# Partials of two weight groups in the attention's PSUM banks, and two half-chunks of attention moved to later units

## The chip, the cores and the metric

One Trainium2 chip, one core of it. The metric is device time in microseconds (us): the median of the runs, of which three are shown for the kernel before. The profile is of one further execution.

## What is computed

The reference, cut to what matters here:

```python
state = alpha[:, :, t, :, None] * state + einsum('bhd,bhe->bhde', k[:, :, t], v[:, :, t])
y[:, :, t] = einsum('bhd,bhde->bhe', q[:, :, t], state)      # 4 x 8 heads, 768 steps, 48 x 48
h = x @ w_in                                                   # 3072 tokens, 384 -> 2048
g = (a0 + a1*h + a2*h2 + a3*h3) / (1 + |b0|*|h| + |b1|*h2 + 1e-6)
x = g @ w_out                                                  # 2048 -> 384
```

After that comes a second network (384 -> 1024 -> 384) with a softmax and a normalisation between its two products. Everything is fp32; each fp32 factor is split into a high and a low part (hi, lo), and a product is three matmuls: hi by hi, hi by lo, lo by hi.

## The kernel before

**Units.** The 768 steps are cut into 6 chunks of 128 steps (512 tokens). The first network runs 16 units per chunk, one for each 128 of the 2048 hidden columns, 96 in all: unit u has chunk c = u // 16 and place f = u % 16. `m_up(u)` (L583) does 9 matmuls (L590) into one of three PSUM banks `hp` and computes the rational function on ScalarE (ACT), VectorE (DVE) and GpSimd (POOL); the last DVE instruction that reads the bank is `fin[u]` (L614 in even units below 24, L621 in the others), and the bank is free for `m_up(u + 3)` after it. `m_down(u - 4)` (L627) does 9 matmuls (L636) into the three `x2p` banks.

**Halves.** Attention is done in 12 halves; half i serves chunk i // 2, columns 256 * (i % 2) of its input `xt`. Halves 0 and 1 are done ahead of unit 0. For a later half, `a_dve(i)` (L300) prepares q and k in six steps on DVE (transposes, two scans, two products) and writes them to DRAM (`qk_d`, `kb_d`); `a_move_qk(i)` (L273) reads them back into `qks`, `a_move(i)` (L279) into `kns`, with v into `vns`. All three of these buffers are single. `a_pe(i)` (L411) then has five steps: scores of the first and of the second pair (L420, a copy on ACT, a triangular mask on POOL L428), y (L444, copied on ACT to the high part and subtracted on DVE to the low part of `xt`, L471), an empty step, and u (L483, with the state's update on DVE L493 and L494). Its scores, y and u come out of the pool `ps_a`, whose tag "at" has two banks. m_up(16), the first unit of chunk 1, needs y of halves 2 and 3.

`half_steps(i)` (L850) takes one step of a_pe(i) and two of a_dve(i + 1), then a_move_qk(i + 1) and the loads of half i + 2, per unit, and ends with a_enter(i + 1). It begins at f = 2 and at f = 10 of every chunk: half 2 at unit 2, half 3 at unit 10, half 4 at unit 18.

**Weights of the first network.** They come in 4 groups (`w1_group`, L550) of 7 pieces: three of `moe_w_in` (128x512 values) and four of `moe_w_out` (128x384). They arrive as 64-bit floats, and `split_w` (L507) turns each piece into fp32 by three integer instructions on DVE: L535 (shift and mask of the high word into the partial `gi`), L538 (sign bit into `gi`), L539 (low word and `gi` into `fi`). ACT then makes the high part (L545) and POOL the low part (L546). Where the partial `gi` lives is `stage["bank"]`:

```python
if stage["bank"] == "x2":
    fp = ps_x2p.tile([128, NTOK], F32, name="fp", tag=f"x2p{x % KT}")
elif stage["bank"] == "at":
    fp = ps_ap.tile([128, NTOK], F32, name="fp", tag="at")
else:
    fp = ft
```

Groups 0 and 1 are done ahead of unit 0 with "x2" (PSUM). Groups 2 and 3 are done beside units 0 to 3 and 4 to 7, two pieces a unit, with the partial in SBUF (`fp = ft`). Their raw words land in two buffers `st`. Group n is first used by m_up(4n). The second network's weights (`w2_split`, 14 pieces, "at") are split one at a time from unit 15 on, at f % 8 of 0 and 7.

**Order.** A planner orders the instructions of each engine when the program is built, and the engines then run them in that order. `issue_after` keeps an instruction behind another one of its engine: `pin(n)` (L842) holds a half's step at unit u behind m_up(u)'s last matmul on TensorE (PE), and behind fin[u - n] on DVE, n = 2. Transfers go through SyncE's queue (SP), in order, and are not pinned.

Of the kernel before, what the change touches and what calls it, by code (L numbers as in the profile page):

```python
# [10 lines left out]
I64 = mybir.dt.int64  # L11
# [12 lines left out]
def _run(*gens):  # L24
    for g in gens:
        for _ in g:
            pass
# [3 lines left out]
def kernel(  # L31
# [23 lines left out]
    NTOK = B * CH  # L55
# [19 lines left out]
    GP = 2  # L75
# [5 lines left out]
    SKIP = (5, 7, 11)  # L81
    AHEAD = 3
    LATE = 2
    U2, IDLE = NF1 - 1, (0, NF1 // 2 - 1)
    assert (B, H, D, CH) == (4, 8, 48, 128)

    const = ctx.enter_context(tc.tile_pool(name="const", bufs=1, side="left"))
# [65 lines left out]
    def network(fast):  # L153
# [38 lines left out]
        def borrow(n, o, dims):  # L192
            if n not in lent:
                lent[n] = moe_pool.tile([128, GW], F32, name=f"lent{n}", tag=f"g{n}")
            size = 1
            for d in dims:
                size *= d
            t = lent[n][:, o:o + size]
            if len(dims) == 1:
                return t  # L200
            nm = "abcd"[:len(dims)]
            return t.rearrange(f"p ({' '.join(nm)}) -> p {' '.join(nm)}", **dict(zip(nm, dims)))
# [197 lines left out]
        def a_prep(i):  # L400
            if i >= NPE:
                yield from a_dve(i)

        def a_enter(i):
            if i < NPE:
                v_load(i)
                yield from a_turn(i)
            else:
                yield from a_move(i)
# [92 lines left out]
        wi = {}  # L502
        wo = {}

        stage = {"n": 0, "wide": False, "bank": None}

        def split_w(src, hi, lo, scale=None):  # L507
            keep = None
            if hi is None:
                keep, raw = lo, moe_pool.tile([128, NTOK], I64, name="st", tag="st", bufs=2)  # L510
                n = src.shape[1]
                both = raw[:].bitcast(F32R)
                hi, lo = both[:, :n], both[:, n:2 * n]
            n = src.shape[1]
            x = stage["n"]
            stage["n"] += 1
            ft = moe_pool.tile([128, NTOK], F32, name="ft", tag="ft", bufs=2)
# [6 lines that stand above are left out]
            if src.dtype == I64:  # L524
                if keep is not None:
                    st = raw
                elif stage["wide"] and x % 6 not in (0, 2):
                    st = borrow(2, 2048 + 1024 * (0, 0, 0, 1, 2, 3)[x % 6], [2 * NTOK]).bitcast(I64)
                else:
                    st = moe_pool.tile([128, NTOK], I64, name="st", tag="st", bufs=2)  # L530
                nc.sync.dma_start(out=st[:, :n], in_=src)
                w32 = st[:, :n].bitcast(I32).rearrange("p (n t) -> p n t", t=2)
                fi = ft[:, :n].bitcast(I32)
                gi = fp[:, :n].bitcast(I32)
                nc.vector.tensor_scalar(  # L535
                    gi, w32[:, :, 1], 3, 0x3FFFFFF8, ALU.logical_shift_left, ALU.bitwise_and
                )
                nc.vector.scalar_tensor_tensor(gi, w32[:, :, 1], -0x40000000, gi, ALU.bitwise_and, ALU.bitwise_or)  # L538
                nc.vector.scalar_tensor_tensor(fi, w32[:, :, 0], 29, gi, ALU.logical_shift_right, ALU.bitwise_or)  # L539
            else:  # L540
                nc.sync.dma_start(out=ft[:, :n], in_=src)
            f = ft[:, :n]
            if scale is not None:
                nc.scalar.activation(f, f, AF.Copy, scale=scale)
            nc.scalar.activation(hi, f, AF.Copy)  # L545
            nc.gpsimd.tensor_tensor(lo, f, hi.bitcast(F32), ALU.subtract)  # L546
            if keep is not None:
                nc.sync.dma_start(out=keep, in_=both[:, :2 * n].bitcast(F32).rearrange("p (x n) -> p x n", x=2))
# [102 lines left out]
        def w2_split():  # L651
            nc.sync.dma_start(out=gln, in_=moe2_g_ln.rearrange("(f p) -> p f", p=128))
            for o in range(0, DF2, 512):
                for kt in range(KT):
                    split_w(moe2_w_in[128 * kt:128 * kt + 128, o:o + 512], None, w2i_d[:, :, kt, o:o + 512])
                    yield
            for f in range(NF2):
                split_w(moe2_w_out[128 * f:128 * f + 128, :], None, w2o_d[:, :, f, :], scale=gln[:, f:f + 1])
                yield
# [144 lines left out]
        if fast:  # L804
            stage["wide"] = True
            stage["bank"] = "x2"
            pre = w1_group(0)
            _run(a_load(0))
            take(pre, PRE[0])
            v_load(0)  # L810
            consts()
            take(pre, PRE[1])
            _run(a_load(1))
            take(pre, PRE[2])
            v_load(1)
            take(pre, PRE[3])
            nc.gpsimd.memset(Sbd, 0.0)
            _run(a_turn(0), a_pe(0), a_turn(1), a_pe(1), pre)
            clear()
            pre = w1_group(1)  # L820
            take(pre, NA)
            _run(a_load(2, ("ra", "rk")))
            with tc.issue_after(marks[0, 1].ins):
                _run(a_prep(2))
            _run(a_move_qk(2))
            _run(a_enter(2), pre)
            _run(a_load(3, ("ra", "rk")))
            stage["wide"] = False
            stage["bank"] = ""
        else:  # L830
            for n in range(NG):
                _run(w1_group(n))
            x_load(0)
# [16 lines left out]
        def half_steps(i):  # L850
            gp = a_pe(i)
            gd = chain(a_prep(i + 1), a_move_qk(i + 1) if i + 1 >= NPE else iter(()), a_load(i + 2, ("ra", "rk")) if i + 2 < NH and i + 1 >= NPE else iter(())) if i + 1 < NH else iter(())
            while True:
                with pin(GP):
                    a = next(gp, "end")
                with pin(GS):
                    b = next(gd, "end")
                    if b != "end":
                        b = next(gd, "end")
                if a == "end" and b == "end":  # L860
                    if i + 1 < NH:
                        _run(a_enter(i + 1))
                        if i + 2 < NH and i + 1 < NPE:
                            _run(a_load(i + 2))
                    return
                yield

        split2 = w2_split() if fast else iter(())
        side = iter(())
        tail = None  # L870
        prep = iter(())
        for u in range(NU + LAG):
            c, f = divmod(u, NF1)
            now[0] = u
            if f % (NF1 // 2) == LATE and u < NU:
                _run(side)
                i = 2 * c + 2 + f // (NF1 // 2)
                side = half_steps(i) if fast and i < NH else iter(())
            if u < NU:
                if f == 0 and c == NCH - 1:  # L880
                    if fast:
                        judge(moe_pool)
                    open2()
                    tail = chain(w2_load("i"), n_load(0), w2_load("o"))
                if f == 0 and c and not fast:
                    x_load(c)
                if fast and u < NF1:
                    if f % 4 == 0:
                        _run(prep)
                        prep = w1_group(f // 4 + 2) if f < 8 else iter(())  # L890
                    with later(G1):
                        take(prep, 1)
                m_up(u)
                if fast and u < NF1:
                    with later(G1):
                        take(prep, 1)
            if u == NU:
                _run(n_load(1))
            take(side, 1)
            if u >= U2 and f % (NF1 // 2) in IDLE:  # L900
                stage["bank"] = "at"
                with later(G2):
                    take(split2, 1)
            if tail is not None:
                _run(split2)
                take(tail, 2)
            if u >= LAG:
                m_down(u - LAG)
            if u - NU + NF1 in EARLY:
                n_tile(EARLY.index(u - NU + NF1))  # L910
                if len(EARLY) == B and u - NU + NF1 == EARLY[-1]:
                    n_turn(0)
# [141 lines left out]
```

## Time and profile before

| | |
|---|---|
| median of 3 runs | 786.02 us (785.37 to 788.82) |
| the profiled execution | 786.76 us, its span 784.9 us |
| PE matmuls busy | 730.2 us, 93% |
| DVE busy | 639.8 us, 82% |
| ACT busy | 534.5 us, 68% |
| POOL busy | 359.9 us, 46% |
| DMA | 101.74 MB, mean 130 GB/s |

Times in the rows are from the start of the span. Unit 0 begins at 56.8 us (its m_up), unit 16 at 169.3. Two instructions of one engine may overlap by some 0.1 us, so that a sum of single durations is a little longer than the busy time.

### The profile page before, as it was taken

How to read it: one execution, taken by the hardware profiler on the slowest of the kernel's cores; microseconds unless marked ns; L12 is line 12 of the kernel's file. 1: busy time of each engine (PE TensorE's matmuls, PEld its weight loads, DVE VectorE, ACT ScalarE, POOL GpSimd, SP SyncE). 2: the span in 40 equal slices, each digit the busy share in tenths (PEclk: the TensorE clock that was granted, in tenths of full speed). 3: DMA queues.
4: the chain of work that ended last, by engine and by line, in shares of the span. 5: the costliest groups of instructions: out<-in, count | busy, mean ns of one | idle time of the engine just before them, and what ended most of it. 6: DMA issues, size and time to landing. Idle time of an engine off the chain costs nothing.

```text
span 784.9 us, 13904 instructions
## 1 busy us (share of the span) xinstructions
PE 730.2 (93%) x4976; PEld 605.3 (77%) x4976; DVE 639.8 (82%) x1110; ACT 534.5 (68%) x983; POOL 359.9 (46%) x306
## 2 busy tenths in 40 slices
PE   4775896999999999999999999999999999999996
PEld 3654674778887788777878788888888989988996
DVE  5999999989899998989898966567887688777640
ACT  2245656779886888788978888788865555555541
POOL 3256677766755344444554433243233433352322
PEclk9767699899999999999999999999999999999998
DMA  7865547373858175536736250640024353542552
GB/s 172 239 201 174 142 154 158 114 182 115 189 167 208 57 196 134 146 83 208 157 121 122 82 121 2 228 175 0 1 82 101 115 120 90 140 102 57 139 121 72
DMA packets 87278, 101.74 MB, mean 130 GB/s; under 512 B 34464, under 2 KB 63136, under 8 KB 87200
## 3 DMA queue, kind: packets, MB, share of 16 engines
q1 hardware_dynamic: 87104, 100.67, 48.5%
q8 instruction: 41, 0.67, 0.4%
q14 instruction: 37, 0.30, 0.1%
q10 hardware_dynamic: 96, 0.10, 0.0%
HBM read 60.59 MB, written 27.56 MB: 112 GB/s over the span
## 4 chain that ended last, share of the span: by engine, by line
DVE 28%; PE 17%; ACT 13%; issue 5%; SPq 4%; DMA 4%; POOL 1%; ACTq 0%; DVEq 0%; POOLq 0%
PE x2p L636 6%; PE hp L590 6%; DVE room L750 3%; SPq L760 3%; DVE room L733 2%; PE op L774 2%; ACT jk L735 2%; DVE p L616 2%; DVE hp L620 2%; DVE w L619 2%; DVE sm L729 2%; DMA room<-room 2%; DMA rq<-in_q_dram 2%; DVE room L748 2%; PE h L710 2%
## 5 line engine op out<-in xcount | busy, mean ns | idle before, releaser
L590 PE MATMUL hp<-xt,g 128*128 128x512 f32 x864 | 225.0, 402 | 9.5 <-DVE alT L302 4.0
L624 POOL TENSOR_TENSOR gl<-p,gh 128x512 fp32r<-128x512 f32 x96 | 127.9, 1332 | 190.2 <-ACT gh L623 104.1
L590 PEld LDWEIGHTS hp<-xt,g 128*128 128x128 f32 x864 | 163.2, 192 | 50.0 <-DVE p L621 5.0
L636 PE MATMUL x2p<-gh,g 128*128 128x512 f32 x576 | 197.5, 397 | 2.8 <-ACT x2e L644 2.1
L636 PEld LDWEIGHTS x2p<-gh,g 128*128 128x128 f32 x576 | 108.6, 189 | 30.5 <-ACT x2e L644 4.7
L636 PE MATMUL x2p<-gl,g 128*128 128x512 f32 x288 | 113.6, 394 | 1.8 <-POOL gl L624 1.8
L774 PE MATMUL op<-w2oh,room 128*128 128x384 f32 x384 | 101.8, 339 | 1.2 <-DVE room L766 0.6
L766 POOL TENSOR_TENSOR room<-room,room 128x1024 fp32r<-128x1024 f32 x22 | 54.6, 2484 | 101.1 <-ACT room L765 79.7
L619 DVE SCALAR_TENSOR_TENSOR w<-w,co,hp 128x512 f32<-128x512 f32 x84 | 62.0, 738 | 44.2 <-ACT hp L618 43.3
L710 PE MATMUL h<-w2ih,x 128*128 128x512 f32 x288 | 90.7, 394 | 0.0
L597 ACT ACTIVATE p<-hp,co 128x512 f32<-128x512 f32 x96 | 65.9, 687 | 13.0 <-POOL gl L624 12.8
L618 ACT ACTIVATE hp<-ah 128x512 f32<-128x512 f32 x84 | 50.1, 596 | 32.8 <-DVE p L616 31.6
L774 PEld LDWEIGHTS op<-w2oh,room 128*128 128x128 f32 x384 | 70.1, 188 | 2.8 <-DVE room L766 1.0
L616 DVE SCALAR_TENSOR_TENSOR p<-p,co,hp 128x512 f32<-128x512 f32 x84 | 61.8, 736 | 10.2 <-ACT p L597 9.9
L598 ACT ACTIVATE w<-ah,co 128x512 f32<-128x512 f32 x96 | 69.4, 724 | 0.7 <-DVE hp L620 0.3
L595 ACT ACTIVATE ah<-hp 128x512 f32<-128x512 f32 x96 | 56.5, 589 | 13.7 <-PE hp L590 13.6
L636 PEld LDWEIGHTS x2p<-gl,g 128*128 128x128 f32 x288 | 54.2, 188 | 15.0 <-POOL gl L624 3.1
L623 ACT ACTIVATE gh<-p 128x512 fp32r<-128x512 f32 x96 | 59.9, 624 | 7.8 <-PE x2p L636 2.7
L774 PE MATMUL op<-w2ol,room 128*128 128x384 f32 x192 | 65.0, 339 | 0.0
L710 PEld LDWEIGHTS h<-w2ih,x 128*128 128x128 f32 x288 | 53.9, 188 | 11.7
L621 DVE SCALAR_TENSOR_TENSOR p<-p,co,hp 128x512 f32<-128x512 f32 x84 | 61.9, 737 | 1.1
L617 ACT ACTIVATE ah<-w,co 128x512 f32<-128x512 f32 x84 | 60.5, 721 | 1.2
(168 smaller groups left out, 1274.8 us busy)
## 6 DMA issues: line engine op xcount, KB each, us to landing
room<-room SPq DMA_DIRECT2D x96, 128.0 KB, 2.4
qk_d<-qk SPq DMA_DIRECT2D x10, 771.0 KB, 4.4
st<-in_moe_w_in_dram SPq DMA_DIRECT2D x15, 512.0 KB, 4.6
st<-in_moe_w_out_dram SPq DMA_DIRECT2D x18, 384.0 KB, 3.5
qks<-qk_d SPq DMA_DIRECT2D x20, 257.0 KB, 5.2
x<-x_d SPq DMA_DIRECT2D x18, 256.0 KB, 3.4
out_dram<-o SPq DMA_DIRECT2D x94, 48.0 KB, 1.6
ra<-in_alpha_dram SPq DMA_DIRECT2D x44, 96.0 KB, 2.3
```

The costliest lines, as they stand in the source:

```text
L590: last["PE", u] = nc.tensor.matmul(hp, lhsT=w[:, kt, 128 * o:128 * o + 128], rhs=xts[c][:, kt, xx, :], start=(kt == 0 and w is hi and xx = ...
L597: nc.scalar.activation(p, hp, AF.Square, bias=co[:, 7:8])
L598: nc.scalar.activation(w, ah, AF.Square, bias=co[:, 6:7])
L616: nc.vector.scalar_tensor_tensor(p, p, a1, hp, ALU.add, ALU.mult)
L617: nc.scalar.activation(ah, w, AF.Ln, bias=rest)
L619: nc.vector.scalar_tensor_tensor(w, w, rest, hp, ALU.add, ALU.mult)
L621: fin[u] = nc.vector.scalar_tensor_tensor(p, p, a0, hp, ALU.add, ALU.mult)
L623: last["ACT", u] = nc.scalar.activation(gh, p, AF.Copy)
L624: last["POOL", u] = nc.gpsimd.tensor_tensor(gl, p, gh[:].bitcast(F32), ALU.subtract)
L636: nc.tensor.matmul(x2ps[c][d], lhsT=w[:, o, 128 * d:128 * d + 128], rhs=gg, start=(f == 0 and w is hi and gg is gh), stop=(f == NF1 - 1 an ...
L710: nc.tensor.matmul(hp[:, 512 * n:512 * n + 512], lhsT=x2s[c][:, kt, x, CH * b:CH * b + CH], rhs=w2[w][:, kt, 512 * n:512 * n + 512], start ...
L774: nc.tensor.matmul(op, lhsT=x[:, 128 * f:128 * f + 128], rhs=w2[w][:, f, :], start=(f == 0 and x is hi and w == "oh"), stop=(f == NF2 - 1 ...
```

## The change

The partials of groups 2 and 3 go to the two "at" banks; group 2's raw words also land in four places of the buffer that group 3 takes later (`borrow(3, ...)`). The steps at units 2 to 11 are written anew (`first_steps`): a_dve(3) goes on one step a unit from unit 2, the scores of half 2 come at units 7 and 8, its y at 9 and its u at 11. Half 3 begins at unit 12 in place of 10, so that its y is at unit 14, its u at 16, and a_dve(4) at units 12 to 14. The second network's splits begin at unit 23 in place of 15.

```diff
-    U2, IDLE = NF1 - 1, (0, NF1 // 2 - 1)
+    FIRST = 10
+    U2, IDLE = NF1 + NF1 // 2 - 1, (0, NF1 // 2 - 1)
...
+                elif stage["near"] and x % 6 not in (0, 2):
+                    st = borrow(3, 2048 + 1024 * (0, 0, 0, 1, 2, 3)[x % 6], [2 * NTOK]).bitcast(I64)
...
-            stage["bank"] = ""
+            stage["near"] = True
+            stage["bank"] = "at"
...
+        def first_steps():
+            gd, gp = a_prep(3), a_pe(2)
+            for n in range(FIRST):
+                if n >= 5:
+                    with pin(GP):
+                        next(gp, "end")
+                with pin(GS):
+                    next(gd, "end")
+                    if n == FIRST - 2:
+                        _run(a_move_qk(3))
+                if n == FIRST - 1:
+                    _run(gp, a_enter(3), a_load(4, ("ra", "rk")))
+                yield
...
-            if f % (NF1 // 2) == LATE and u < NU:
+            if f in ((LATE, LATE + FIRST) if c == 0 else (LATE, LATE + NF1 // 2)) and u < NU:
                 _run(side)
                 i = 2 * c + 2 + f // (NF1 // 2)
-                side = half_steps(i) if fast and i < NH else iter(())
+                side = iter(()) if not fast or i >= NH else first_steps() if i == 2 else half_steps(i)
...
                     if f % 4 == 0:
                         _run(prep)
+                        if f:
+                            stage["near"] = False
                         prep = w1_group(f // 4 + 2) if f < 8 else iter(())
...
             if u >= U2 and f % (NF1 // 2) in IDLE:
-                stage["bank"] = "at"
                 with later(G2):
                     take(split2, 1)
```

## Rows read from the trace of the kernel before

**Rows 1.** The page's 40 slices: PE and DVE busy tenths, granted clock.

```profile
PE   4775896999999999999999999999999999999996
DVE  5999999989899998989898966567887688777640
PEclk9767699899999999999999999999999999999998
```

**Rows 2.** Windows, all engines: us, busy of PE, PEld, DVE, ACT, POOL, PEclk, DMA, GB/s.

```profile
56.80:169.30 112.50, 91.86 (x655) 70.69 (x656) 108.99 (x167) 71.59 (x133) 77.28 (x63) 0.86 0.57 153
169.30:600.00 430.70, 424.36 (x2995) 342.12 (x2994) 363.67 (x586) 353.47 (x638) 196.08 (x176) 1.00 0.45 122
```

**Rows 3.** Timeline of PE: start us, us, what, idle before and its releaser.

```profile
80.88 2.04 PE L420 MATMUL sc<-qks 48*128 48x128 f32 x8 [10.74 <-DMA qks<-qk_d]
...
109.21 1.14 PE L483 MATMUL u<-vns,kns 128*64 128x48 f32 x32
...
136.75 4.21 PE L590 MATMUL hp<-xt,g 128*128 128x512 f32 x9 [4.02 <-DVE alT L302]
...
153.85 1.13 PE L444 MATMUL y<-A,vns 128*32 128x128 f32 x31
...
169.34 2.22 PE L590 MATMUL hp<-xt,g 128*128 128x512 f32 x9
```

**Rows 4.** Timeline of DVE, the same columns.

```profile
67.38 0.40 DVE L535 TENSOR_SCALAR ft<-st 128x512 int32<-128x512 int32 x1
...
74.61 1.11 DVE L496 TENSOR_TENSOR Sbd<-u,end 48x384 f32<-48x384 f32 x2
...
79.91 0.68 DVE L614 SCALAR_TENSOR_TENSOR p<-w,hp 128x512 f32<-128x512 f32 x1
...
84.15 0.34 DVE L535 TENSOR_SCALAR ft<-st 128x384 int32<-128x384 int32 x1
...
136.02 0.67 DVE L614 SCALAR_TENSOR_TENSOR p<-w,hp 128x512 f32<-128x512 f32 x1
...
157.39 0.66 DVE L290 STREAM_TRANSPOSE qk<-rq 128x256 f32<-128x256 f32 x1
...
159.97 1.01 DVE L471 TENSOR_TENSOR xt<-y,xt 128x512 fp32r<-128x512 f32 x2
```

**Rows 5.** Windows of lines 535, 538, 539 in turn: us, DVE busy, PEclk, DMA, GB/s.

```profile
67.38:136.69 69.31, 9.17 (x12) 0.87 0.63 166
...
67.38:136.69 69.31, 12.92 (x12) 0.87 0.63 166
...
67.38:136.69 69.31, 11.83 (x12) 0.87 0.63 166
```

**Rows 6.** Groups by form, DVE, 160 to 460 us: busy us, mean ns, idle before.

```profile
L538 DVE SCALAR_TENSOR_TENSOR fp<-st,fp 128x384 int32<-128x384 int32 x8 | 4.5, 559 | 0.2
L535 DVE TENSOR_SCALAR fp<-st 128x384 int32<-128x384 int32 x8 | 4.5, 558 | 0.2
L539 DVE SCALAR_TENSOR_TENSOR ft<-st,fp 128x384 int32<-128x384 int32 x8 | 4.4, 552 | 0.2
L535 DVE TENSOR_SCALAR fp<-st 128x512 int32<-128x512 int32 x6 | 4.1, 691 | 0.5 <-DMA st<-in_moe_w_in_dram 0.4
L538 DVE SCALAR_TENSOR_TENSOR fp<-st,fp 128x512 int32<-128x512 int32 x6 | 4.1, 690 | 0.1
L539 DVE SCALAR_TENSOR_TENSOR ft<-st,fp 128x512 int32<-128x512 int32 x6 | 4.1, 682 | 0.1
```

**Rows 7.** Timeline of SP's queue: start us, us, issue.

```profile
118.66 0.43 SPq L348 DMA_DIRECT2D vns<-in_v_dram  x1
...
163.80 1.72 SPq L276 DMA_DIRECT2D qks<-qk_d  x4
```

**Rows 8.** DMA issues: queue, KB each, median us from issue to landing.

```profile
qks<-qk_d SPq DMA_DIRECT2D x20, 257.0 KB, 5.2
...
vns<-in_v_dram SPq DMA_DIRECT2D x22, 192.0 KB, 6.2
```

More of the change, by code (lines that the diff above doesn't have):

```diff
@@ L503, in network @@
         wo = {}
-        stage = {"n": 0, "wide": False, "bank": None}
+        stage = {"n": 0, "wide": False, "near": False, "bank": None}
         def split_w(src, hi, lo, scale=None):
```

## The prediction

> **What bounds the kernel now.** I begin with the slices. From the second on PE is below 9 tenths until about the eighth, while DVE stands at 8 or 9 all along; behind that PE is at 9 until the end [rows 1]. The windows make this sharper. From m_up(0) to m_up(16) PE is busy for 91.9 of 112.5 us at a mean granted clock of 0.86 (a mix of 1.2 and 2.4 GHz), DVE for 109.0. From there to 600 us PE is busy for 424.4 of 430.7 us at full clock [rows 2]. So the ramp in front of unit 16 is DVE's, and what follows is PE's. A microsecond taken out of the ramp moves everything behind it; one taken off DVE later moves next to nothing, and I cost it at nothing.
>
> Where does DVE hold PE up? The timeline of PE has two long gaps. The first, 10.74 us before 80.88, is put down to the transfer that brings half 2's q and k [rows 3]. It looks like the stall that this change removes, but it is worth little: the next unit in the queue, m_up(3), needs the bank of unit 0, whose fin[0] (L614) runs from 79.91 to 80.6 [rows 4]. Without the transfer PE would stand until 80.6 all the same. The second gap, 4.02 us, ends at 136.75 with m_up(11) [rows 3]. It needs the bank of unit 8, and fin[8] ends at 136.7 [rows 4]: DVE again. From there on PE is almost gapless, since m_up(11) to m_up(16) take 32.6 us. So the ramp has two parts: up to fin[8] DVE's queue sets the time, after it PE's work does.
>
> **The change part by part.** *The partials.* Between 67.38 us and fin[8], 12 of the 14 pieces of groups 2 and 3 are split: six of 512 values, six of 384. The three lines take 9.17 + 12.92 + 11.83 = 33.9 us there [rows 5]. With the partial in PSUM the later w2 pieces, of the same shapes and types, take 0.691 + 0.690 + 0.682 = 2.06 us at 512 and 0.558 + 0.559 + 0.552 = 1.67 at 384 [rows 6]. Six of each: 12.4 + 10.0 = 22.4 us. That is **11.5 us less** on the engine that sets this part, and I take all of it, because DVE is busy for 97% of the ramp [rows 2]. The bounds: 0, if DVE merely idles where it was busy; and 11.5 and the 4.0 us gap and the 3 to 4 us that PE runs at half clock behind it (m_up(11) takes 4.21 us, m_up(16) 2.22 [rows 3]), together some 19. The two pieces after fin[8] lie beside PE's own work: nothing.
>
> Here a rule speaks against the change. The row first: an SBUF L535 that meets no delay takes 0.40 us at 512 and 0.34 at 384 [rows 4], less than the 0.691 and 0.558 in PSUM [rows 6]; but the twelve of the ramp took 9.17 us, 0.76 each [rows 5], so most were held up. By the fast rows alone L535 would have been 6 x 0.40 + 6 x 0.34 = 4.4 us and becomes 7.5, 3.1 longer in place of 1.7 shorter, and the sum would be 11.5 - 4.8 = 6.7. That is a rival below. The Trainium skill, "VectorE: DVE Perf Modes", section "Why PSUM operands drop a tier", states that a PSUM operand keeps a one-input instruction out of the mode that uses both SBUF read ports. These rows agree, but they also show that here the mode was mostly not had.
>
> *Scores, y and u of half 2 to units 7 to 11.* PE's work is the same. PE alone would not be the bound: from 70.1 us to m_up(11) it has 8 up and 7 down units of 2.2 us [rows 3], 33 us, and half 2's small matmuls. These are at most 8 us of scores (32 at the half-clock rate of 8 in 2.04), 4 of y (112 at 31 in 1.13) and 1 of u. So 46 us at the most, up to 116, before 136.7 - 11.5 = 125.2. Half 2's y and state update on DVE (L471, 1.01 us [rows 4], and L493) come about at fin[8] in place of before it: 0 to 2 us of gain, counted as 0. a_dve(3), one step a unit, still ends at unit 7, before fin[8]: nothing. Its qk transfer has until unit 12: nothing.
>
> *The "at" banks.* Two banks now serve the splits beside half 1's last tiles, which are let go by L496 at 74.61 to 75.7 [rows 4]; the first split of group 2 was at 67.38. If it had to wait for L496, DVE would lose up to 7 us, filled in part by units 0 and 1. Usually one of the two banks is free: I take 0, bound 7.
>
> *Raw words in four more places.* Group 2's loads go out earlier. DVE had no lack of work: 0.
>
> *Half 3 two units later.* Three transfers get closer to their readers, and PE's queue is in order, so a wait there holds all the matmuls behind it. A unit of PE is 4.4 us (two nines at 2.2).
> - xt for m_up(16): before, y ended at 155.0 [rows 3] and the low part on DVE at 161.0 [rows 4], 6.0 us later. Now m_down(10), m_up(15) and m_down(11) lie between, 6.6 us: 0, bound 4 if DVE is late.
> - v for y(3): u(2) ended at 110.35 [rows 3], the second vns transfer was issued at 118.66 [rows 7] and takes 6.2 [rows 8], so 125.3, 15 us later. Now three units and the scores lie between, 13.2 + 2.3 = 15.5 us: 0, bound 5.
> - q and k for half 4's scores, at unit 18 as before while a_dve(4) has moved by two units: its last transposes ended at 158.0 [rows 4], the qks issues at 165.5 [rows 7], and landing takes 5.2 [rows 8]: 170.7, 12.7 us. DVE ended a_dve(4) two units behind its place in the code; two units behind unit 14 is m_up(16), and up to the scores PE has two units, u(3) and m_up(18): 8.8 + 1.1 + 2.2 = 12.1 us. **A wait of about 1 us**, bounds 0 and 10.7, what the half-2 scores waited [rows 3].
>
> *w2 splits from unit 23.* They leave units 15 and 16 and end at unit 72, before their readers at unit 80: work moved under PE's, 0.
>
> **Sum.** -11.5 + 1 = -10.5 us. The profiled execution took 786.76 us, 0.74 above the median of the three runs, so 776.3 of its kind, 775.5 against the median.
>
> **The rivals.**
> 1. *More comes back.* The gap at m_up(11) and the half clock behind it shrink as well, and half 2's y and u leave the part before fin[8]: -19 us, 767. For: PE's bound is 9 us below DVE's. Against: DVE has 97% of the ramp, and a shorter queue on it idles more.
> 2. *The tier.* L535's delay is only handed on to the next instruction with two SBUF operands (the scans, L320), so 6.7 us come off, less the 1: 780. For: the fast L535 rows. Against: the w2 pieces run beside POOL work too. The rule is the one of the Trainium skill, "VectorE: DVE Perf Modes", section "Why PSUM operands drop a tier".
> 3. *Given back, or not done.* Banks not free (7), or the two waits at y(3) and unit 16 (5 and 4): 11.5 is met by 7 to 11.5 and the time is 783 to 786. For: lead times of 15 us against 15.5. Against: no unit after 16 shows such waits with the usual distances.
> 4. *Slower: scores wait for their transfer, twice.* The scores of half 3 at unit 12 and of half 4 at unit 18 each stand as long as half 2's did, 10.74 us, with all later units behind them in PE's queue: 21.5 - 11.5 = +10, 796. It decides from where both waits exceed 11.5 us together. For: that wait did happen at the one place where the transfer had no lead, and half 4 loses two units of lead. Against: half 3 has five units between a_dve(3) and its scores.
>
> **How the numbers follow.** Chances: the forecast 0.50, rival 1 0.15, rival 2 0.10, rival 3 0.14, rival 4 0.11. The range from 764 to 784 holds the forecast's own 771 to 780, rivals 1 and 2 and the lower part of 3; the rest and rival 4 are left out. A measurement of this kernel can tell a change of about 0.5%, 3.9 us: faster is below 782.1. Forecast, rivals 1 and 2 and a little of 3 are faster, 0.78; most of 3 is the same, 0.12; 4 is slower, 0.10, but for its mildest part.
>
> **What would show it.** Right: lines 535, 538 and 539 of all 28 pieces at 1.7 and 2.1 us a piece; DVE's busy time in the ramp about 12 us shorter; fin[8] at about 125 and m_up(16) near 159 us; from there to the end the same length as before. Scores of half 4 with a wait of a microsecond or so. Wrong: L538 and L539 at 0.7 us but DVE idle before them; waits on qks, vns or xt of more than 3 us at units 12 to 18; m_up(16) earlier and the stretch behind it longer.

## The result: 0.8% slower, and the profile after

Over ten runs each the median is 792.88 us after the change and 786.2 before; the ratio is **1.0082, with a 95% interval of 1.006 to 1.0104**. The forecast was 775.5 us. The profiled execution took 793.11 us, its span 791.3. In the changed file lines are one to three higher: L538, L541 and L542 are the split's three instructions, L421 the scores, L445 y, L471 and L472 the high and low part of xt, L593 m_up, L639 m_down, L598 ACT's first instruction of a unit.

The page of the changed kernel, its span and slices, against [rows 1]:

```profile
span 791.3 us, 13930 instructions
...
PE   4776879998999999999999989999999999999996
...
DVE  5999999808889999889898966566887698777630
```

PE's seventh slice went from 6 to 9 and its sixth from 9 to 7. DVE's ninth slice, from 158 to 178 us, went from 8 to 0: DVE stands nearly still on both sides of m_up(16). The windows of the changed kernel (us; busy of PE, PEld, DVE, ACT, POOL; PEclk, DMA, GB/s) have PE a little busier and DVE less busy in the first 169.3 us [rows 2]. I cut the ramp at m_up(11) and m_up(16):

```profile
56.80:169.30 112.50, 95.11 (x580) 75.60 (x583) 96.96 (x163) 76.35 (x138) 72.43 (x66) 0.89 0.44 121
...
56.80:124.09 67.29, 51.23 (x213) 40.84 (x214) 65.54 (x113) 45.67 (x82) 44.93 (x38) 0.82 0.47 134
124.09:172.80 48.71, 46.69 (x444) 37.07 (x442) 31.44 (x52) 31.33 (x59) 27.87 (x29) 1.00 0.41 114
```

DVE's busy time in the old ramp's window went from 109.0 to 97.0 us, in part because it stands idle at the end of that window. But from m_up(11) to m_up(16) it now takes 48.7 us in place of 32.6, and DVE is busy for 31.4 of them. It was busy for nearly all of it before:

```profile
136.75:169.34 32.59, 31.02 (x254) 23.95 (x255) 31.12 (x51) 24.41 (x46) 22.13 (x20) 0.92 0.52 142
```

The table gives the start of ACT's first instruction of a unit (us; in brackets the difference from the kernel before), read off each trace; the last three columns are experiments that come below.

```
unit   before   after            e1               e6               e10
  4     96.0     86.9 ( -9.1)     86.6 ( -9.4)     86.0 (-10.0)     86.9 ( -9.1)
  8    126.0    114.6 (-11.5)    115.3 (-10.8)    110.7 (-15.3)    114.5 (-11.5)
 12    152.7    133.1 (-19.6)    140.2 (-12.5)    141.3 (-11.4)    135.7 (-17.1)
 14    164.8    144.7 (-20.1)    153.0 (-11.8)    151.0 (-13.7)    147.3 (-17.5)
 16    173.6    178.4 ( +4.8)    167.7 ( -5.9)    160.4 (-13.1)    176.2 ( +2.6)
 32    254.8    259.8 ( +5.0)    249.9 ( -4.9)    243.4 (-11.4)    257.7 ( +2.9)
 68    444.2    446.6 ( +2.4)    440.3 ( -3.9)    433.6 (-10.6)    448.5 ( +4.3)
 76    481.3    488.4 ( +7.2)    478.4 ( -2.8)    471.9 ( -9.3)    487.1 ( +5.9)
 95    576.2    583.3 ( +7.2)    573.1 ( -3.0)    566.5 ( -9.6)    581.7 ( +5.6)
```

The change was 20 us ahead at unit 14 and 5 us behind at unit 16. What happened between? First the waits of DVE and PE from 56.8 to 215 us, longest first (waited for: total, times, longest):

```profile
DVE xt L472 <- ACT xt L471: 14.2, 1, 14.2
...
PE sc L421 <- DMA qks<-qk_d: 1.0, 1, 1.0
```

One wait of 14.2 us: the next instruction in DVE's order is the low part of half 3's y, which needs ACT's copy of that y. The chain of waits of the changed kernel shows what that y was waiting for:

```profile
147.67 0.66 DVE qk L291
149.17 1.46 SPq L267
152.57 5.00 DMA qks<-qk_d
157.86 1.28 POOL gl L627
159.18 4.15 PE x2p L639 x17
163.34 1.64 PE sc L421 x16
164.97 2.28 PE x2p L639 x9
167.25 1.08 PE sc L421 x8
168.34 3.83 PE y L445 x108
172.17 0.59 ACT xt L471
172.80 5.54 PE hp L593 x23
```

Half 3's q and k arrive at 157, its scores follow up to 168, y up to 172, and m_up(16) begins at 172.8. The transfer could not go before half 2's y, the last reader of the single buffer qks, ended at 149.4 us; SP's queue, still at another load (L267, in the chain above), issued it at 151.2. Half 2's y was late because half 2's scores were late. Timeline of SP's queue, of DVE and of PE in the changed kernel:

```profile
148.70 2.41 SPq L267 DMA_DIRECT2D ra<-in_alpha_dram  x3
151.22 1.77 SPq L277 DMA_DIRECT2D qks<-qk_d  x4
```

```profile
94.39 0.68 DVE L538 TENSOR_SCALAR fp<-st 128x512 int32<-128x512 int32 x1
...
123.70 0.55 DVE L542 SCALAR_TENSOR_TENSOR ft<-st,fp 128x384 int32<-128x384 int32 x1
...
128.66 0.55 DVE L542 SCALAR_TENSOR_TENSOR ft<-st,fp 128x384 int32<-128x384 int32 x1
```

```profile
124.09 2.20 PE L593 MATMUL hp<-xt,g 128*128 128x512 f32 x9
...
129.62 1.16 PE L421 MATMUL sc<-qks 48*128 48x128 f32 x8
...
148.23 1.13 PE L445 MATMUL y<-A,vns 128*32 128x128 f32 x31
```

Group 3 is split from 94.4 to 129.2 us. Half 2's first scores, whose place in the code is unit 7, begin at 129.62, right behind the last of these splits and behind m_up(11). Both want the two "at" banks. The sixth of the seven splits ends at 124.2 us, the seventh at 129.2. PE was not idle between 124.1 and 129.6, so the trace of the change does not tell a wait for a bank in these last 5 us from the order of PE's queue, which was fixed when the program was built. The experiments have to do that.

### The profile page after: what moved, and what is told of

The parts are those of the page before. It is cut to its first block, busy times and chain, and to the rows that moved or that the text cites. A ratio compares the mean times of both kernels' runs of the same rounds, so it can differ in the third digit from the quotient of the medians.

```text
span 791.3 us, 13930 instructions
## 1 busy us (share of the span) xinstructions
PE 738.0 (93%) x4976; PEld 614.9 (78%) x4976; DVE 626.0 (79%) x1110; ACT 534.1 (67%) x983; POOL 354.6 (45%) x306
## 4 chain that ended last, share of the span: by engine, by line
PE 49%; DVE 26%; ACT 9%; DMA 5%; issue 5%; SPq 3%; POOL 1%; DVEq 0%; ACTq 0%; POOLq 0%
PE h L713 13%; PE op L777 12%; PE hp L593 11%; PE x2p L639 10%; DVE w L622 2%; DVE hp L623 2%; DVE p L624 2%; DVE p L619 2%; DVE qk L291 2%; ACT p L600 2%; DVE alT L318 2%; DVE alT L325 2%; DVE fp L541 1%; ACT w L601 1%; DMA lent<-in_moe_w_out_dram 1%
## 5 line engine op out<-in xcount | busy, mean ns | idle before, releaser
L593 PE MATMUL hp<-xt,g 128*128 128x512 f32 x864 | 228.8, 409 | 23.9 <-DVE p L624 11.3
L593 PEld LDWEIGHTS hp<-xt,g 128*128 128x128 f32 x864 | 166.5, 196 | 65.5 <-DVE p L624 13.9
L639 PE MATMUL x2p<-gh,g 128*128 128x512 f32 x576 | 193.6, 395 | 0.7 <-ACT x2e L647 0.7
L639 PEld LDWEIGHTS x2p<-gh,g 128*128 128x128 f32 x576 | 109.0, 189 | 25.2 <-ACT x2e L647 1.5
L639 PE MATMUL x2p<-gl,g 128*128 128x512 f32 x288 | 113.7, 395 | 1.7 <-POOL gl L627 1.7
L598 ACT ACTIVATE ah<-hp 128x512 f32<-128x512 f32 x96 | 56.8, 592 | 27.6 <-PE hp L593 25.3
L639 PEld LDWEIGHTS x2p<-gl,g 128*128 128x128 f32 x288 | 54.0, 188 | 14.9 <-POOL gl L627 2.9
```

What stands on the lines that cost most here:

```text
L593: last["PE", u] = nc.tensor.matmul(hp, lhsT=w[:, kt, 128 * o:128 * o + 128], rhs=xts[c][:, kt, xx, :], start=(kt == 0 and w is hi and xx = ...
L639: nc.tensor.matmul(x2ps[c][d], lhsT=w[:, o, 128 * d:128 * d + 128], rhs=gg, start=(f == 0 and w is hi and gg is gh), stop=(f == NF1 - 1 an ...
```

## The experiments

**The theory** (the "bank theory" below). The banks of a tag are given out in the order in which the code asks. Group 3's seven partials are asked for at units 4 to 7, ahead of half 2's scores, so those wait for the last of them; half 3 stands behind half 2, and m_up(16) behind half 3. **Rivals:** the moved places by themselves are too late; or the loss is the second network's later splits. Each experiment has 4 to 12 runs and one trace. Medians and ratios below are against runs of the kernel before on the same chip (785.6 to 785.8 us).

**e1, group 3's partials back in SBUF.**

```diff
                         if f:
                             stage["near"] = False
+                            stage["bank"] = ""
...
             if u >= U2 and f % (NF1 // 2) in IDLE:
+                stage["bank"] = "at"
```

> The change, but group 3's partials back in SBUF; group 2's stay in the two at banks, all moved places stay. Bank theory (half 2's scores take the at banks in turn behind group 3's last partial, which is let go only at 129 us, and half 3's chain then reaches m_up(16) late): scores of half 2 begin at 103 to 110 us in place of 129.6, m_up(16) at 155 to 165 us in place of 172.8, the time is 776 to 785. Place rival (y of half 3 at unit 14 is too close to unit 16 by itself): m_up(16) still not before 168 us, the time is 790 or more. Split rival (the loss is the second network's splits moved to units 23 to 72): m_up(16) may move, but the time stays at 788 to 793.

785.68 us, ratio 0.9992 (0.9969 to 1.0015): 7 us below the change. The scores' row in e1 (duration of one; first and last start):

```profile
L421 PE MATMUL sc<-qks x80: 272/272/374, 102.8 to 175.0; 48*128 48x128 f32 x80
```

They begin at 102.8 us in place of 129.6, though nothing of the attention was touched. The bank theory's mark is met. m_up(16) begins at 162.8 us, inside its range (the table's 167.7 is ACT's first instruction); the time is 0.7 us above its range. One thing is left over: from unit 14 to 16 e1 still gives back 6 of its 12 us.

**e2, the second network's splits from unit 15 again.** `U2, IDLE = NF1 - 1, ...`

> The change, but the second network's splits begin at unit 15 again. Bank theory: the ramp is as in the change (m_up(16) at 170 to 178 us); some 3 to 5 us are regained between units 68 and 76, where the change loses them, and up to 4 are lost at units 15 to 24: 788 to 793. Split rival: all of the loss goes, 784 to 787. Place rival: 790 to 793.

791.44 us, 1.0065 (1.0046 to 1.0085). The later splits are not the loss. The trace shows the trade: e2 is 8.1 us behind the kernel before at unit 16, 3.3 more than the change, and some 10 at units 68 and 76 alike, while the change goes from +2.4 to +7.2 there.

**e3, the banks alone:** `stage["bank"] = "at"` in the kernel before, halves and second splits where they were.

> The kernel before with the at banks for groups 2 and 3 and nothing else: halves 2 and 3 and the second network's splits at their old places. Bank theory: half 2's scores are held behind the partials here too, y of half 3 comes after all the m_downs of chunk 0, m_up(16) at 168 to 176 us, the time is 786 to 794. Place rival: without the move nothing is late, DVE's 11.5 us come off: 773 to 778. Split rival: the same, 773 to 778.

791.52 us, 1.006 (1.0037 to 1.0084), with the halves at their old, earlier places. Scores begin at 97.2 us in place of 80.9 [rows 3], m_up(16) at 174.5, and the same wait of DVE is there:

```profile
DVE xt L471 <- ACT xt L470: 7.6, 1, 7.6
```

So the banks do the harm without the move.

**e5, the move alone:** the change with `stage["bank"] = ""` for both groups, "at" for the second network's splits. The four more places for raw words stay too.

> The change with the partials of groups 2 and 3 in SBUF as before: only the moved halves, splits and raw words. Bank theory: half 2's scores come at their own place (103 to 112 us), DVE has its 12 us again, m_up(16) at 165 to 173 us, the time is 784 to 791. Place rival: as slow as the change or slower, 792 to 800. Split rival: 790 to 794.

787.36 us, 1.0019 (0.9992 to 1.0045): no difference that can be measured. Scores begin at 105.3 us, at their place in the code. Without the banks the moved places, splits and raw words together neither hurt nor help.

**e10, the banks' turn against the code's place:** the change with `FIRST = 8` and `if n >= 3`, so that half 2's scores are at units 5 and 6 in the code and half 3 begins at unit 10 again.

> The change with all partials of groups 2 and 3 in the at banks, but the steps of half 2 two units earlier in the code (scores at units 5 and 6) and half 3 from unit 10. Bank theory: the banks' turn and not the code's place sets the order, so u of half 2 still comes behind the last partial and y of half 3 behind all the m_downs of chunk 0; m_up(16) at 168 to 176 us, time 788 to 794. Place rival: two units earlier in the code is two units earlier on the chip: m_up(16) at 155 to 163 us, 776 to 784.

794.31 us, 1.011 (1.0083 to 1.0137), 0.3 us above the bank theory's range. Two units earlier in the code, the scores begin at 120.0 us, behind the fourth of group 3's partials, which ends at 118.0 (DVE's timeline, then the scores' row):

```profile
117.43 0.54 DVE L542 SCALAR_TENSOR_TENSOR ft<-st,fp 128x384 int32<-128x384 int32 x1
```

```profile
L421 PE MATMUL sc<-qks x68: 272/272/373, 120.0 to 179.9; 48*128 48x128 f32 x68
```

Four is also the number that the code asks for ahead of these scores. Half 2's u comes behind the last partial and half 3's y behind all the m_downs of chunk 0; m_up(16) begins at 172.2. The place rival falls.

**e12, a dose:** the change with group 3's last four pieces in SBUF (`elif stage["bank"] == "at" and not (fast and 24 <= x < 28)`).

> The change, but only group 3's first three pieces use the at banks; its last four, of w_out, are back in SBUF. Bank theory, as a dose: half 2's scores begin right behind the last partial that is left in a bank, about 110 to 118 us, between 102.8 (none of group 3) and 129.6 (all seven); m_up(16) between 166 and 172 us, the time 784 to 790. Place rival: m_up(16) and the time as in the first experiment, 784 to 787, with the scores at 103 to 106 us.

784.61 us, 0.9977 (0.9947 to 1.0007). In e12 (DVE's timeline, then the scores' row) the first scores begin within 0.1 us of the end of the second of three partials, 107.53 + 0.69 = 108.2 us:

```profile
107.53 0.69 DVE L542 SCALAR_TENSOR_TENSOR ft<-st,fp 128x512 int32<-128x512 int32 x1
```

```profile
L421 PE MATMUL sc<-qks x80: 272/272/373, 108.3 to 174.0; 48*128 48x128 f32 x80
```

That is the sharpest of the runs: none of group 3 in the banks, scores at 102.8; three, 108.3; seven, 129.6. It is 2 us before the range that I gave, because with two banks the first scores need only the bank that comes free first, and PE stood idle for 3.4 us up to them. m_up(16), at 162.7 us, also came 3 us before its range.

**e6, a version that beats both:** e1 with `FIRST = 8` and `if n >= 3`.

> The first experiment's kernel (group 2's partials in the at banks, group 3's in SBUF) with the steps of half 2 two units earlier (scores at units 5 and 6, y at 7, u at 9) and half 3 from unit 10 again, as before. If what that kernel still lost at unit 16 (11.8 us ahead of the kernel before at unit 14, 5.9 at unit 16) is the place of half 3's y two units ahead of its reader, the lead is kept: unit 16 8 to 12 us earlier than before, the time 775 to 781. If the loss is PE's and DVE's own work catching up, unit 16 stays 4 to 7 us earlier: 781 to 786.

**777.69 us, 0.9901 (0.9877 to 0.9925).** Half 3's y now ends at 147.5 us and m_up(16) begins at 158.1:

```profile
146.35 1.13 PE L445 MATMUL y<-A,vns 128*32 128x128 f32 x31
...
158.14 2.20 PE L593 MATMUL hp<-xt,g 128*128 128x512 f32 x9
```

The lead of 13.7 us at unit 14 is kept at unit 16 (13.1). So the 6 us that e1 gave back lie in these two units. That it is half 3's y so close to its reader is argued, since e6 moves half 2's steps as well. For it: in e1 this y ends at 157.9 us, ACT copies it only from 162.1, and PE stands three times, 1.9 us in all, at the start of m_up(16); in e6 it does not stand there.

**e7, e6 with the second network's splits from unit 15.**

> The same with the second network's splits from unit 15 again. If DVE still binds behind unit 16, two splits more at units 15 and 16 cost 2 to 4 us there and units 68 to 76 give 2 to 4 back: the same time as its neighbour within 2 us. If the later place costs by itself, 2 to 4 us less than its neighbour.

777.88 us, 0.99 (0.9874 to 0.9925): the same. The two places are worth the same.

**e11, e6 with group 2's partials in SBUF as well.**

> The fast version (half 2 at units 5 to 9, half 3 from unit 10, group 3 in SBUF) with group 2's partials in SBUF too: no partial in PSUM behind unit 0. If the gain of the fast version is DVE's (seven pieces, about 6 us at the two prices), 5 to 7 us of it go: 782 to 785. If it comes from the moved steps alone, the time stays at 777 to 779; if all of it is the banks, 786 and more.

788.86 us, 1.0027 (1.0007 to 1.0048). Without the banks of group 2 nothing of e6's gain is left: 11 us of the median hang on seven pieces whose price difference is about 6. The traces place most of it. At unit 95 e6 is 9.6 us ahead of the kernel before and e11 0.2 behind, so 9.8 us arise ahead of the second network. The three instructions of group 2's pieces take 12.7 us in e6 and 18.1 in e11, 5.5 more; those of group 3's, in SBUF in both, take 17.5 and 20.9, another 3.4. Why group 3's are dearer in e11 is open. PE's longest wait for DVE is 11.1 us in e11 and 8.0 in e6.

**e13, e6 without the four more places for raw words** (`stage["near"] = False`).

> The fast version without the four more places for group 2's raw words. If the banks' turn rules, pieces that arrive later let the banks go later, half 2's scores come 3 us or more later and unit 16 loses 4 to 8 us: 781 to 786. If the raw words' places cost and bring nothing, as the prediction had it: 777 to 779.

783.75 us, 0.9985 (0.9958 to 1.0012): 6 us of e6's 8 are gone, and so are 6 of its 13 at unit 16. The two rows are of DVE's waits in e13, and none is longer than 0.9 us on these transfers in e6:

```profile
DVE fp L538 <- DMA st<-in_moe_w_out_dram: 2.2, 1, 2.2
DVE fp L538 <- DMA st<-in_moe_w_in_dram: 1.8, 1, 1.8
```

Group 2's last partial ends at 105.2 us in place of 91.6, half 2's scores begin at 94.5 in place of 92.0 (2.5 us, a little less than expected), and its y ends at 119.0 in place of 105.9. I had costed these places at nothing. This run also sets a limit to the theory: the scores begin 0.1 us behind the sixth of group 2's seven partials (DVE's timeline, then PE's) and ahead of the seventh, which the code asks for earlier. They need the first bank that comes free, not the last partial:

```profile
93.86 0.53 DVE L542 SCALAR_TENSOR_TENSOR ft<-st,fp 128x384 int32<-128x384 int32 x1
```

```profile
94.48 1.13 PE L421 MATMUL sc<-qks 48*128 48x128 f32 x8 [1.23 <-issue]
```

**e8, the kernel before with group 2's first three partials in the x2p banks,** which are idle until m_down(0): `if stage["bank"] == "x2" or fast and 14 <= x < 17`.

> The kernel before with the partials of group 2's first three pieces in the three x2p banks, which nothing uses until m_down(0); nothing else changed. Bank theory: no tile of the attention stands behind these partials, so the saving of the three pieces (9.9 us in the profile of before against 6.2 at the PSUM price, 3.7 us) comes through, 781 to 784. If a partial in PSUM gains nothing by itself: 785 to 788. If m_down(0) is held behind them as the scores were: 786 or more.

788.55 us, 1.0029 (1.0015 to 1.0044). In its trace unit 95 is 2.6 us earlier than before, so most of the 3.7 us came through the first network. The time lies in the range of the last branch, but units 4 and 8 are 3.7 and 4.9 us earlier than before, so m_down(0) was not held. The span is 785.1 against 784.9: the second network took 3 us longer. The lead is there up to 636 us and is lost at small instructions of DVE that read two SBUF tiles. Three of them, L745 to L747, take 2.1 to 2.3 us each in e8. In the kernel before the middle one takes 0.16, because it starts just ahead of POOL's instruction and not just behind (POOL and DVE in e8, then in the kernel before):

```profile
640.41 2.42 POOL L766 TENSOR_TENSOR room<-room,room 128x1024 fp32r<-128x1024 f32 x1
...
640.50 2.34 DVE L746 SCALAR_TENSOR_TENSOR sm<-sm 128x1 f32<-128x1 f32 x1
```

```profile
642.79 2.40 POOL L766 TENSOR_TENSOR room<-room,room 128x1024 fp32r<-128x1024 f32 x1
...
642.75 0.16 DVE L746 SCALAR_TENSOR_TENSOR sm<-sm 128x1 f32<-128x1 f32 x1
```

From there DVE's softmax runs at the same time in both kernels. Near the end PE waits 2.6 us for it in e8, and then has a granted clock of 0.5 for some 3 us. The profiled executions of e5 and e11 lose 2 to 3 us in the same stretch of the second network, so a few us between two medians say little about the ramp. The time of e8 is inconclusive about the price.

## Why the prediction was wrong

**Right: the partials' price and DVE's part of the ramp.** The 14 pieces of the changed kernel (windows of lines 542, 541, 538; us, DVE busy):

```profile
67.60:129.30 61.70, 8.37 (x14) 0.86 0.48 135
...
67.60:129.30 61.70, 8.48 (x14) 0.86 0.48 135
...
67.60:129.30 61.70, 8.60 (x14) 0.86 0.48 135
```

25.4 us; the prices of [rows 6] give 22.4 for twelve [rows 5] and 25.7 for all. The gap at m_up(11) went as well, so that it began at 124.1 in place of 136.75 us: 12.7 against the 11.5 of the sum. The wait of half 4's scores, costed at 1 us, was 1.0; that is luck, since this place was reached some 14 us later than forecast (m_up(16) at 172.8 in place of 159). The tier rival did not show in the sum: L538 took 0.61 us on average, less than the 0.76 of SBUF [rows 5]. Its row is real all the same: in e11, where group 2's L538 in SBUF met no delay, the seven took 2.7 us, and 4.3 in e6 with the partial in PSUM; the other two instructions give back more than that (15.5 against 8.4).

**Wrong: "Two banks now serve the splits beside half 1's last tiles ... I take 0, bound 7."** This step failed. It asked who stands ahead of the splits in the tag, and never who stands behind them. Half 2's scores do, with its y and u behind them, and I wrote of them only that PE's work is the same and that DVE's is not later. They came at 129.6 us, and through qks, half 3's scores and its y that stretched m_up(11) to m_up(16) from 32.6 to 48.7 us: 16.1 us, with one wait of 14.2 on DVE. Adding group 3's banks to e1 costs 7 us of the median, to e6 (that is e10) 17.

**Too small: "xt for m_up(16) ... 0, bound 4."** I counted the units between y and its reader from the code. e1 against e6 prices these two units at 7 us at unit 16, half 2's steps being moved with them.

**Wrong premise: "what follows is PE's."** The windows gave PE 98.5% busy behind unit 16 [rows 2]. When the changed kernel reached m_up(16) PE had done all 16 m_downs of chunk 0, 3.7 more than before at that point, some 7.5 us of its work (2.04 us each). By the end none of it had come back: 4.8 us behind at unit 16, 7.2 at unit 95. The chain of the kernel before from 216 to 300 us, by line, would have said so, for PE is not in it:

```profile
by line: issue 13.3%; DMA rq<-in_q_dram 7.2%; DVE p L616 6.5%; DVE hp L620 5.4%; ACT p L597 5.2%; ACT hp L618 4.9%; ACT gh L623 4.4%; DVE w L619 4.0%; DVE p L621 3.5%; DVE alT L324 3.2%; POOL gl L624 3.1%; ACT w L598 3.1%; ACT ah L617 3.0%;
```

The premise is right further on: from 444 to 576 us, units 68 to 95, the same chain of the kernel before is PE's for 90%. Up to there the chain is mostly DVE's and ACT's, so PE's work done ahead was of no use and DVE's idle time of 14 us at unit 16 was lost. It is also why the later splits of the second network, costed at 0, show in the trace as a gain around unit 16 and a loss at units 68 to 76; their sum was 0 within the intervals (e2, e7).

**The rivals.** The slower one had its sign right and its mechanism wrong: it had the scores wait for their transfer at units 12 and 18. What scores waited for was a bank, at a place that I had called free.

## What to carry to other kernels

When a temporary is put into a tag with few buffers, list what asks for that tag behind it in the code, not only ahead of it: whoever comes later waits until the temporaries have let a bank go, on whatever engine it runs. If the chain behind has a fixed reader (here the first unit of a chunk), the temporaries nearest to it are the ones to leave out: with one group of two in the banks and the chain two units earlier the same idea gains 1% in place of losing 0.8%. And a high busy share of PE does not make it the bound; see, stretch by stretch, whether the chain runs through it.

## What I had not expected of the hardware

A DVE instruction that reads two SBUF tiles can cost what is left of a GpSimd instruction that began ahead of it. In e8 L746, on 128x1 values, begins 0.09 us behind POOL's L766 and ends with it, 2.34 us later; in the kernel before it begins 0.04 us ahead of one and takes 0.16. The split's second instruction reads two SBUF tiles when the partial is in SBUF: for group 2's pieces it took 0.55 to 2.12 us in e11, and 0.53 to 0.70 in e6 with the partial in PSUM. The bank spares it the long times, while its shortest time stays about the same. That the splits are held by POOL as L746 is, is argued: no run took POOL's work away.
